# Attention outputs in five circulating PSUM banks, and the clamp of the first 24 weight tiles on GpSimd

## The chip, the cores and the metric

The kernel runs on one core of a Trainium2 chip, as one launch. The metric is the device time of that core in microseconds (us), the median of three runs.

## What is computed

The reference, cut to its core (NumPy, float32 inputs except where noted below):

```python
# attention: batch 4, heads 8, 512 local tokens, 32 global tokens, head size 64, window 32
def sm(s):
    e = np.exp(s - np.max(s, axis=-1, keepdims=True))
    return e / (np.sum(e, axis=-1, keepdims=True) + 1e-09)
s_g = scale * q_g @ concat(k_g, k_l).T            # a global token sees everything
out_g = sm(s_g) @ concat(v_g, v_l)
s_ll = where(abs(pos_q - pos_k) <= 32, scale * q_l @ k_l.T, -1e9)
s_l = concat(scale * q_l @ k_g.T, s_ll)           # a local token sees its window and the globals
out_l = sm(s_l) @ concat(v_g, v_l)
x = heads_to_columns(concat(out_g, out_l))        # 2176 tokens x 512
h = max(x @ w1, x @ w2, x @ w3)                   # 512 -> 768
x = h @ w_out                                     # 768 -> 512
g = softplus(x @ w_in2)                           # 512 -> 2048
out = g @ w_out2                                  # 2048 -> 512
```

The weights are float64 arrays. The kernel reads them as pairs of 32-bit integers, puts them together into float32 on the chip ("decoding"), and then splits each float32 number into a high part that TensorE multiplies exactly and a low remainder (high and low part of weights: the two halves of `w`; of activations: `xh` and `xl`, `hh` and `hl`). A product is three matmuls: high x high, high x low, low x high.

## The kernel before

**Attention** runs in 32 chunks k, each of two heads and 256 local tokens. A chunk goes through these steps: `s1`, the scores on TensorE into a PSUM tile of two banks (`ps`, L149) and on VectorE the masked row maximum, kept as a minimum of the negated scores (L155), which also takes the scores out of PSUM; `s1e`, the exponentials on ScalarE (L162); `s1f`, the reciprocal of the sums on VectorE (L168, L169) and two normalising multiplies on GpSimd (L171, L172); `s1g`, for every other chunk, the scores of the global tokens (L184, L190); `s2`, five transposes of the attention weights on TensorE (L218, L219); `s2e`, their copies out of PSUM (L230 on ScalarE; L232 on ScalarE or L234 on VectorE); `s3`, the attention output (L245, L249); `s3h` and `s3l`, its high and low part (L259, L270) or, from the third half-batch on, a copy that goes to memory (L262). `gsoft` is the softmax of the global tokens (L202 to L208), `g2` the transposes of their weights with the copies (L279 to L285), `g3` their output (L297).

**The first dense pair** runs in eight units u of 256 or 288 tokens. A unit has 18 **up slots**: 12 matmuls each (L504 to L506) of one weight tile with `xh` and `xl`, then a copy (L515, ScalarE) or a running maximum (L518, VectorE). After three slots `split_h` makes the parts `hh` (L533) and `hl` (L536). Two **down blocks** of 36 matmuls each follow (L550 to L552). The two products of the second pair come after all of it, from about 320 us on.

**Decoding** a tile of 128 x 512 weights (`dec_stream`) takes an absolute value on ScalarE (L448), a clamp on VectorE (L462), and three integer steps on VectorE (L465, L469, L473), the first two of which write a PSUM tile `pt` as long as the tile is "staged", which the first 24 are. Then ScalarE copies the high part (L442) and GpSimd subtracts for the low part (L443).

**PSUM.** The pool `pm` has five banks that circulate: up slots, down blocks, transposes, global scores and `pt` all take the next one. The scores have two banks, and the attention outputs `po` and `pog` share one bank of their own (tag "o", L241, L292).

**Order.** Every engine works through its instructions in program order, and the program order is what the Python code writes: `att_stream` and `dec_stream` are generators that the code at L671 to L715 advances. Each yield of attention is followed by some steps of decoding (`part`, with the debts `D0`, `D2`, `D3`) and by an up slot if its weights are decoded; after that the up slots of units 0 and 1 run with `FJ` decoding steps and `RJ` attention steps each, and from unit 2 on with `RA` attention steps a slot. For the first `KS` = 8 chunks a chunk is written as one fixed sequence (L328 to L362), for the later ones ("dense attention", among up slots) as the sequence of letters in `ORD` (L364 to L404), with a yield after nearly every step. All loads from memory are issued by SyncE in the order in which the code reaches them.

## Time and profile before

| | before |
|---|---|
| median of three runs | 813.41 us (811.31 to 814.13) |
| the profiled execution | 813.12 us, its span 811.4 us |
| TensorE matmul busy | 778.8 us, 96% of the span |
| VectorE, ScalarE, GpSimd busy | 524.2 us (65%), 423.7 us (52%), 173.6 us (21%) |
| chain of work that ended last | TensorE 86%, VectorE 6%, ScalarE 3%, memory 2% |

Busy time is counted over the whole span. The program has stages with different limits: eleven attention chunks with the first decoding (to 66.5 us), the up slots of the first two units with the rest of the 24 tiles (to 119.8 us), attention and down blocks (to 155.5 us), dense attention between up slots (to about 320 us), and the dense products. The mean granted clock of TensorE over the span is 0.994 of its full speed.

### The profile page before, as it was taken

Reading aid. Unit: us, or ns where it says so; the run is one execution under the profiler, and the core shown is the slowest. Engines: PE = TensorE matmul, PEld = TensorE weight load, DVE = VectorE, ACT = ScalarE, POOL = GpSimd, SP = SyncE. Lnnn points to the kernel's source line nnn. Section 1 sums busy time; section 2 is a strip of 40 time slices with the busy share of each in tenths; the row PEclk is TensorE's granted clock in tenths of the full one; section 3 lists DMA queues with packets and bytes.
Section 4 is the critical chain, followed back from the end, with each engine's and each line's share of the span. In section 5 each row is a group of like instructions: output and inputs, shape, how many; then the busy total and the mean of one; then the engine's idle time right before and its main releaser. Section 6 shows DMA issues by size and latency. Waiting matters only on the chain.

```text
span 811.4 us, 17312 instructions
## 1 busy us (share of the span) xinstructions
PE 778.8 (96%) x6600; PEld 730.4 (90%) x6600; DVE 524.2 (65%) x1350; ACT 423.7 (52%) x1032; POOL 173.6 (21%) x183
## 2 busy tenths in 40 slices
PE   5689988999999999999998999999999999999998
PEld 3578987988989998999998889988999999999998
DVE  5867962455454453377746455655437989999996
ACT  5744534433433441324322688888878744444443
POOL 4434533211211120022223033433312200000000
PEclk9999999999999999999999999999999999999999
DMA  9827314433433411526020445544625734444421
GB/s 339 311 87 256 148 53 123 141 123 101 147 108 112 153 48 48 205 107 214 15 65 15 165 151 170 179 158 155 210 88 179 247 95 130 130 131 130 130 80 65
DMA packets 72403, 111.89 MB, mean 138 GB/s; under 512 B 9984, under 2 KB 51840, under 8 KB 72320
## 3 DMA queue, kind: packets, MB, share of 16 engines
q1 hardware_dynamic: 72320, 110.78, 40.8%
q8 instruction: 52, 0.85, 0.4%
q14 instruction: 31, 0.25, 0.1%
HBM read 80.67 MB, written 30.08 MB: 136 GB/s over the span
## 4 chain that ended last, share of the span: by engine, by line
PE 86%; DVE 6%; ACT 3%; DMA 2%; issue 1%; POOL 0%; SPq 0%; DVEq 0%; ACTq 0%; POOLq 0%
PE pu L504 8%; PE ph L976 8%; PE ph L978 8%; PE ph L977 8%; PE pu L505 7%; PE pu L506 7%; PE mb L863 7%; PE mb L864 7%; PE mb L862 7%; PE pd L550 3%; PE pd L551 3%; PE pd L552 3%; PE ps L149 2%; ACT s L162 2%; PE po L245 2%; DMA raw<-in_w_dram 2%
## 5 line engine op out<-in xcount | busy, mean ns | idle before, releaser
L504 PE MATMUL pu<-xh,w 128*128 128x288 f32 (+1 forms) x576 | 172.3, 299 | 5.3 <-DVE tmp L473 4.8
L505 PE MATMUL pu<-xl,w 128*128 128x288 f32 (+1 forms) x576 | 167.4, 291 | 0.0
L506 PE MATMUL pu<-xh,w 128*128 128x288 f32 (+1 forms) x576 | 166.7, 289 | 0.0
L863 PE MATMUL mb<-wo,oh 128*128 128x256 f32 x480 | 135.8, 283 | 0.0
L864 PE MATMUL mb<-wo,ol 128*128 128x256 f32 x480 | 135.7, 283 | 0.0
L862 PE MATMUL mb<-wo,oh 128*128 128x256 f32 x480 | 135.2, 282 | 0.0
L504 PEld LDWEIGHTS pu<-xh,w 128*128 128x128 f32 x576 | 109.6, 190 | 11.0 <-issue 5.4
L976 PE MATMUL ph<-o,w 128*128 128x384 f32 (+1 forms) x320 | 115.2, 360 | 0.5 <-ACT o L555 0.5
L978 PE MATMUL ph<-o,w 128*128 128x384 f32 (+1 forms) x320 | 115.0, 360 | 0.0
L977 PE MATMUL ph<-o,w 128*128 128x384 f32 (+1 forms) x320 | 115.0, 359 | 0.0
L505 PEld LDWEIGHTS pu<-xl,w 128*128 128x128 f32 x576 | 109.8, 191 | 0.0
L506 PEld LDWEIGHTS pu<-xh,w 128*128 128x128 f32 x576 | 109.6, 190 | 0.0
L984 DVE SCALAR_TENSOR_TENSOR g<-ph,a 128x384 f32<-128x384 f32 (+1 forms) x80 | 48.8, 610 | 88.5 <-ACT a L983 64.0
L855 ACT ACTIVATE oh<-sm 128x640 fp32r<-128x640 f32 (+1 forms) x72 | 49.8, 692 | 89.6 <-DVE sm L850 83.8
L862 PEld LDWEIGHTS mb<-wo,oh 128*128 128x128 f32 x480 | 91.7, 191 | 0.0
L864 PEld LDWEIGHTS mb<-wo,ol 128*128 128x128 f32 x480 | 91.3, 190 | 0.0
L863 PEld LDWEIGHTS mb<-wo,oh 128*128 128x128 f32 x480 | 91.2, 190 | 0.0
L162 ACT ACTIVATE s<-s,nm 128x160 f32<-128x160 f32 x128 | 53.4, 419 | 56.4 <-DVE nm L155 56.3
L443 POOL TENSOR_TENSOR w<-tmp,w 128x512 fp32r<-128x512 f32 x40 | 53.1, 1328 | 128.9 <-ACT w L442 82.5
L518 DVE TENSOR_TENSOR m<-m,pu 128x256 f32<-128x256 f32 (+1 forms) x96 | 41.7, 434 | 56.4 <-PE pu L506 50.6
L171 POOL TENSOR_TENSOR s<-s,rs 128x512 f32<-128x512 f32 x32 | 33.4, 1044 | 165.1 <-DVE rs L169 87.8
L976 PEld LDWEIGHTS ph<-o,w 128*128 128x128 f32 x320 | 60.2, 188 | 6.5 <-ACT o L555 0.7
(125 smaller groups left out, 1584.7 us busy)
## 6 DMA issues: line engine op xcount, KB each, us to landing
gl<-gd SPq DMA_DIRECT2D x32, 512.0 KB, 5.1
kq<-in_kq_dram SPq DMA_DIRECT2D x31, 448.0 KB, 4.4
raw<-in_w_out_dram SPq DMA_DIRECT2D x22, 512.0 KB, 4.1
raw<-in_w_dram SPq DMA_DIRECT2D x18, 512.0 KB, 7.6
gd<-g SPq DMA_DIRECT2D x48, 192.0 KB, 2.5
vt<-in_vw_dram SPq DMA_DIRECT2D x16, 512.0 KB, 5.5
raw<-in_w_in_dram SPq DMA_DIRECT2D x16, 512.0 KB, 7.5
gd<-g SPq DMA_DIRECT2D x32, 256.0 KB, 3.9
```

Source lines behind the costliest of these rows:

```text
L162: nc.scalar.activation(s[:, u, :], s[:, u, :], AF.Exp, scale=-1.0, bias=g["nm"][:, u:u + 1], accum_out=g["sm"][:, u:u + 1])
L443: nc.gpsimd.tensor_tensor(w[:, 1, :], tf, w[:, 0, :].bitcast(F32), op=ALU.subtract)
L504: nc.tensor.matmul(p, lhsT=w[:, 0, k], rhs=xh[:, k, 0:n], start=(k == 0), stop=False)
L505: nc.tensor.matmul(p, lhsT=w[:, 0, k], rhs=xl[:, k, 0:n], start=False, stop=False)
L506: nc.tensor.matmul(p, lhsT=w[:, 1, k], rhs=xh[:, k, 0:n], start=False, stop=(k == 3))
L855: nc.scalar.activation(oh[:, a:b], src, AF.Copy)
L862: nc.tensor.matmul(p, lhsT=oh[:, a], rhs=w[:, 0], start=st, stop=False, skip_group_check=True)
L863: nc.tensor.matmul(p, lhsT=oh[:, a], rhs=w[:, 1], start=False, stop=False, skip_group_check=True)
L864: nc.tensor.matmul(p, lhsT=ol[:, a], rhs=w[:, 0], start=False, stop=sp, skip_group_check=True)
L976: nc.tensor.matmul(p, lhsT=w[:, 0, k], rhs=oh[:, 0:n], start=(k == 0), stop=False)
L977: nc.tensor.matmul(p, lhsT=w[:, 0, k], rhs=ol[:, 0:n], start=False, stop=False)
L978: nc.tensor.matmul(p, lhsT=w[:, 1, k], rhs=oh[:, 0:n], start=False, stop=(k == 3))
```

## The change

- `po` and `pog` take the next of the five circulating banks instead of a bank of their own; the bank that this frees becomes a pool `pt` for the decoding's PSUM tile alone.
- The clamp of the 24 staged tiles runs on GpSimd, right behind the absolute value. The other 16 tiles keep theirs on VectorE. A staged tile has three yields instead of four.
- The fixed sequence holds for eleven chunks instead of eight (`KS`), and its steps stand in another order: the reciprocals and multiplies of chunk k-1 behind the scores of chunk k, the global softmax in one piece but for its scaling, and `g2` and `g3` apart from their copies (`g2e`, `g3e`).
- Dense attention is written out instead of `ORD`: scores, output and transposes directly behind one another, then the exponentials, the multiplies, and the global tokens' steps.
- `hl` runs on GpSimd for the first three tiles of unit 0 alone; before, for all of units 0 and 1.
- The numbers that set how many steps of one stream go with one of the other are set anew (two pieces of that table are shown). `warm` is removed; it was called with 0.

```diff
-    WM = 0
     KL = 10
     KW = 9
-    KS = 8
-    ORD = 'AHaBbFDIEG'
+    KS = 11
     HHA = 2
-    HLP = 2
+    HLP = 3
...
+    pt = mo_ctx.enter_context(tc.tile_pool(name="pt", bufs=1, space=PSUM))
...
-        po = pp.tile([128, 4, 64], F32, tag="o", name="po", bufs=1)
+        po = ptile([128, 4, 64], "po")
...
-        nc.vector.tensor_copy(gt[0:96, 4, :], pb[0:96])
...
+        c["gt"], c["p"] = gt, (pa, pb)
+
+    def g2e(b, s):
+        c = gs[b, s]
+        gt, (pa, pb) = c["gt"], c["p"]
+        nc.vector.tensor_copy(gt[0:96, 4, :], pb[0:96])
         nc.scalar.activation(gt[:, 0:3, :], pa[:, 0:384].rearrange("p (c n) -> p c n", n=128), AF.Copy)
         nc.vector.tensor_copy(gt[0:64, 3, :], pa[0:64, 384:512])
-        c["gt"] = gt
...
     def g3(b, s):
-        c = gs.pop((b, s))
...
-        po = pp.tile([128, 2, 32], F32, tag="o", name="pog", bufs=1)
+        po = ptile([128, 2, 32], "pog")
...
+        c["po"] = po
+
+    def g3e(b, s):
+        po = gs.pop((b, s))["po"]
...
-            soft = iter(())
-            if 1 <= k <= n and groups[k - 1][1] == 1 and groups[k - 1][2] % 2 == 1:
-                soft = gsoft()
+            gq = None
+            if 2 <= k < n + 2 and groups[k - 2][1] == 1 and groups[k - 2][2] % 2 == 1:
+                gq = groups[k - 2][0], groups[k - 2][2] // 2
...
                 if q2 is not None:
                     s2(q2)
                     p2 += 1
+                for c in late:
+                    g3(*c)
                 s1e(k, 0)
                 s1e(k, 1)
                 if q3 is not None:
                     s3h(q3)
+                if k:
+                    s1f(k - 1)
+                next(soft, None)
+                if q2 is not None:
+                    s2e(q2)
+                if gq:
+                    g2(*gq)
+                elif gpend:
+                    soft = gsoft()
+                    next(soft)
+                    next(soft)
                 yield 2 if k > 1 else 4
-                next(soft, None)
                 if q3 is not None:
                     s3l(q3)
                     p3 += 1
-                if q2 is not None:
-                    s2e(q2)
-                s1f(k)
-                next(soft, None)
-                if late:
-                    g3(*late.pop())
-                    ng += 1
                 if k % 2 == 1:
                     s1g(k)
-                next(soft, None)
-                if k >= 2:
-                    b, hf, pr = groups[k - 2]
-                    if hf == 1 and pr % 2 == 1:
-                        g2(b, pr // 2)
-                        late.append((b, pr // 2))
-                yield 3
+                for c in late:
+                    g3e(*c)
+                    ng += 1
+                late = []
+                if gq:
+                    g2e(*gq)
+                    late.append(gq)
+                yield 3 if k else 4
...
             else:
-                for c in ORD:
-                    if c in "AaBb":
-                        if k < n:
-                            (s1 if c in "AB" else s1e)(k, "AaBb".index(c) // 2)
...
-                    elif c == "D":
-                        while p3 < p2 and p3 <= k - 2:
-                            s3(p3)
-                            s3h(p3)
-                            s3l(p3)
-                            p3 += 1
-                            yield 0
-                    elif c == "F":
...
-                    elif c == "E":
-                        while p2 <= min(k - 1, n - 1):
-                            s2(p2)
-                            s2e(p2)
-                            p2 += 1
-                            yield 0
...
+                if k == KS:
+                    s1f(k - 1)
+                if k < n:
+                    s1(k, 0)
+                    s1(k, 1)
+                while p3 < p2 and p3 <= k - 2:
+                    s3(p3)
+                    s3h(p3)
+                    s3l(p3)
+                    p3 += 1
+                while p2 <= min(k - (2 if k == KS else 1), n - 1):
+                    s2(p2)
+                    s2e(p2)
+                    p2 += 1
+                yield 0
+                for i in range(2):
+                    if k < n:
+                        s1e(k, i)
+                        yield 0
+                    next(soft, None)
+                    next(soft, None)
+                if k < n:
+                    s1f(k)
+                for c in late:
+                    g3(*c)
+                if gq:
+                    g2(*gq)
+                if k < n and k % 2 == 1:
+                    s1g(k)
...
+                if gpend:
+                    soft = gsoft()
+                yield 0
...
             t = tmps[i] = dp.tile([128, 512], I32, tag="tmp", name="tmp", bufs=3)
-            nc.scalar.activation(t.bitcast(F32), raws[i][:, :, 1].bitcast(F32), AF.Abs)
+            tf = t.bitcast(F32)
+            nc.scalar.activation(tf, raws[i][:, :, 1].bitcast(F32), AF.Abs)
+            if staged:
+                nc.gpsimd.tensor_scalar(tf, tf, F_LO, F_HI, op0=ALU.max, op1=ALU.min)
...
-            nc.vector.tensor_scalar(tf, tf, F_LO, F_HI, op0=ALU.max, op1=ALU.min)
-            yield
-            t2 = ptile([128, 512], "pt").bitcast(I32) if staged else t
+            if not staged:
+                nc.vector.tensor_scalar(tf, tf, F_LO, F_HI, op0=ALU.max, op1=ALU.min)
+                yield
+            t2 = pt.tile([128, 512], F32, tag="t", name="t2").bitcast(I32) if staged else t
...
-        (nc.gpsimd if HLP > u else nc.vector).tensor_tensor(hl[:, f, 0:n], m, hh[:, f, 0:n].bitcast(F32), op=ALU.subtract)
+        (nc.gpsimd if u == 0 and f < HLP else nc.vector).tensor_tensor(hl[:, f, 0:n], m, hh[:, f, 0:n].bitcast(F32), op=ALU.subtract)
...
-        FJ = 2.3
-        AD = 5
-        D0 = 0.5
-        D2 = 2.0
-        D3 = 1.0
+        FJ = 1.75
+        AD = 3
...
-        RD = 2.0
-        RA = 1.9
+        RD = 1.4
+        RA = 1.35
...
-            if v == 2:
+            elif v == 2:
                 flush()
-                part(D2)
-            elif v == 4:
-                continue
+                part(D2 if cnt < 8 else D2L)
             elif v == 3:
-                part(D3 if cnt > 1 else 3.0)
-                for _ in range(NS):
+                part(D3 if cnt < 8 else D3L)
+                for _ in range(NS if cnt < 8 else NSL):
                     if au[0] and ready(0):
                         slot(0)
-            else:
-                part(D0)
-                if cnt > 8 and au[0] and ready(0):
-                    flush()
-                    slot(0)
-            cnt += 1
+                cnt += 1
```

The instructions of each engine, in program order, before and after, at the places on which the steps below rest (without row numbers). From about 320 us on TensorE's order is the same in both.

VectorE, at the program's start, from the last of chunk 0's row maxima on, before (`s` and `nm` are what a row maximum writes, `rs` the reciprocals, L462 is the clamp of the first weight tile, the last row chunk 1's row maximum):

```order
L155 ISA s,nm<-ps,mask 128x160
L155 ISA nm 128x1
L168 TENSOR_SCALAR rs<-sm 128x4
L169 RECIPROCAL rs<-rs 128x4
L462 TENSOR_SCALAR tmp<-tmp 128x512
L155 ISA s,nm<-ps,mask 128x160
```
and after, from the last of chunk 2's row maxima on (L148, L161, L162 are the lines of before's L155, L168, L169; `t_254` is the decoding's PSUM tile, L475 the first shift):

```order
L148 ISA s,nm<-ps,mask 128x160
L148 ISA nm 128x1
L161 TENSOR_SCALAR rs<-sm 128x4
L162 RECIPROCAL rs<-rs 128x4
L475 TENSOR_SCALAR t_254<-tmp 128x512
L148 ISA s,nm<-ps,mask 128x160
```
The clamp is gone from VectorE, the first decoding step there is the shift, and 18 more rows (the row maxima of chunks 1 and 2, and a pair of reciprocals) stand ahead of it.

GpSimd, among the up slots of the first two units, before (L443 is the low part of a decoded tile `w`, L536 the low part `hl` of a hidden tile, L171 an attention multiply):

```order
L536 TENSOR_TENSOR hl<-m,hh 128x256
L443 TENSOR_TENSOR w<-tmp,w 128x512 x3
L536 TENSOR_TENSOR hl<-m,hh 128x256
L443 TENSOR_TENSOR w<-tmp,w 128x512 x4
L171 TENSOR_TENSOR s<-s,rs 128x4x128
```
and after (L449 is L443, L457 the clamp, L546 is L536):

```order
L449 TENSOR_TENSOR w<-tmp,w 128x512
L457 TENSOR_SCALAR tmp<-tmp 128x512
L449 TENSOR_TENSOR w<-tmp,w 128x512
L457 TENSOR_SCALAR tmp<-tmp 128x512
L546 TENSOR_TENSOR hl<-m,hh 128x256
L449 TENSOR_TENSOR w<-tmp,w 128x512
L457 TENSOR_SCALAR tmp<-tmp 128x512
```
Between two subtracts there now stands a clamp, of the tile that comes two later.

GpSimd before, around the low parts of the second unit:

```order
L171 TENSOR_TENSOR s<-s,rs 128x4x128
L172 TENSOR_TENSOR sg<-s,rs 128x128
L171 TENSOR_TENSOR s<-s,rs 128x4x128
L172 TENSOR_TENSOR sg<-s,rs 128x128
L536 TENSOR_TENSOR hl<-m,hh 128x288 x6
L171 TENSOR_TENSOR s<-s,rs 128x4x128
```
and VectorE after, where these six now stand (L227 copies transposed attention weights, L114 is the low part of a later unit's input):

```order
L148 ISA s,nm<-ps,mask 128x160
L148 ISA nm 128x1
L227 COPY pwt<-pw 128x512
L546 TENSOR_TENSOR hl<-m,hh 128x288 x6
L161 TENSOR_SCALAR rs<-sm 128x4
L162 RECIPROCAL rs<-rs 128x4
L114 TENSOR_TENSOR xl<-xr,xh 128x256 x2
```
The six low parts have moved from GpSimd, behind two chunks' multiplies, to VectorE, behind one copy.

TensorE, dense attention, before (`pw`, `pg` transposes, `ps` scores, `pu` an up slot):

```order
L218 MATMUL pw<-ident,s 128x128 x4
L219 MATMUL pg<-ident,sg 128x128
L149 MATMUL ps<-kq 64x160 x8
L504 MATMUL pu<-xh,w 128x256
L505 MATMUL pu<-xl,w 128x256
L506 MATMUL pu<-xh,w 128x256
```
and after (`po` is the output of the chunk before the one whose scores are `ps`; L142, L238, L242, L211, L212 are the lines of before's L149, L245, L249, L218, L219):

```order
L142 MATMUL ps<-kq 64x160 x8
L238 MATMUL po<-pgt,vb 64x128 x4
L242 MATMUL po<-pwt,vt 64x64 x8
L211 MATMUL pw<-ident,s 128x128 x4
L212 MATMUL pg<-ident,sg 128x128
L514 MATMUL pu<-xh,w 128x256
L515 MATMUL pu<-xl,w 128x256
```
Before, transposes and scores stood together and the output four up slots later; now scores, output and transposes stand in one row ahead of the slots.

## Rows read from the trace of the kernel before

**Rows 1.** Stretches: length, busy PE, PEld, DVE, ACT, POOL (count), clock, DMA, GB/s

```profile
0.00:66.50 66.50, 47.97 (x632) 38.12 (x633) 44.95 (x173) 40.36 (x142) 26.88 (x43) 0.97 0.64 232
66.50:119.80 53.30, 48.50 (x363) 47.49 (x361) 45.31 (x86) 24.58 (x50) 27.43 (x24) 0.97 0.44 165
119.80:155.50 35.70, 32.90 (x353) 28.91 (x352) 12.22 (x54) 16.82 (x62) 10.32 (x14) 0.95 0.36 112
155.50:320.00 164.50, 163.13 (x1890) 147.69 (x1887) 80.20 (x301) 64.43 (x231) 24.82 (x34) 1.00 0.34 108
320.00:811.40 491.40, 486.33 (x3372) 468.18 (x3370) 341.48 (x740) 277.54 (x548) 84.14 (x68) 1.00 0.41 134
68.20:69.61 1.41, 1.41 (x14) 1.41 (x13) 1.34 (x3) 1.41 (x4) 1.02 (x2) 1.00 0.77 206
155.53:157.15 1.62, 1.62 (x16) 1.48 (x13) 1.14 (x9) 1.01 (x5) 0.00 (x0) 1.00 0.47 133
280.50:282.13 1.63, 1.63 (x15) 1.49 (x14) 0.69 (x1) 0.28 (x2) 1.25 (x2) 1.00 0.75 255
```

**Rows 2.** TensorE's waits, 0 to 160 us: waiter, releaser, sum, count, longest

```profile
PE ps L149 <- DVE nm L155: 5.4, 3, 2.2
PE pu L504 <- DVE tmp L473: 4.8, 4, 2.2
...
PE pd L551 <- POOL hl L536: 2.0, 1, 2.0
```

**Rows 3.** VectorE groups by shape, 0 to 120 us: busy, mean ns, idle before

```profile
L469 DVE SCALAR_TENSOR_TENSOR pt<-raw,pt 128x512 int32<-128x512 int32 x24 | 16.6, 691 | 0.4
...
L155 DVE CUSTOM_DVE_ANT_0 s<-ps,mask 128x160 f32<-128x160 f32 x44 | 11.8, 319 | 6.9 <-PE ps L149 6.9
L462 DVE TENSOR_SCALAR tmp<-tmp 128x512 f32<-128x512 f32 x24 | 10.3, 427 | 5.1 <-ACT tmp L448 5.1
...
L518 DVE TENSOR_TENSOR m<-m,pu 128x288 f32<-128x288 f32 x10 | 4.5, 447 | 0.0
```

**Rows 4.** GpSimd groups by shape, 0 to 120 us

```profile
L443 POOL TENSOR_TENSOR w<-tmp,w 128x512 fp32r<-128x512 f32 x24 | 30.9, 1289 | 35.3 <-ACT w L442 30.7 <-issue 4.6
...
L65 POOL COPY mask<-mask 128x160 f32<-128x160 f32 x1 | 0.3, 320 | 0.0
```

**Rows 5.** GpSimd's timeline: start, length, instruction, wait before it

```profile
12.47 1.04 POOL L171 TENSOR_TENSOR s<-s,rs 128x512 f32<-128x512 f32 x1 [3.16 <-DVE rs L169]
```

**Rows 6.** Chain of waits, 0 to 20 us: start, length, instruction

```profile
9.46 0.43 DVE tmp L462
...
10.16 1.76 ACT s L162 x8
```

**Rows 7.** TensorE's timeline, score matmuls of two early chunks

```profile
10.96 1.34 PE L149 MATMUL ps<-kq 64*64 64x160 f32 x16 [2.17 <-DVE nm L155]
...
31.86 0.78 PE L149 MATMUL ps<-kq 64*64 64x160 f32 x16 [0.66 <-PE pg L219]
```

**Rows 8.** ScalarE groups by shape, 0 to 120 us

```profile
L448 ACT ACTIVATE tmp<-raw 128x512 f32<-128x512 f32 x24 | 15.9, 661 | 9.9 <-DMA raw<-in_w_dram 5.2 <-DMA raw<-in_w_out_dram 4.6
L442 ACT ACTIVATE w<-tmp 128x512 fp32r<-128x512 f32 x24 | 15.0, 625 | 10.3 <-DVE tmp L473 10.3
```

**Rows 9.** VectorE's timeline: last decoding step of two weight tiles

```profile
66.47 0.66 DVE L473 SCALAR_TENSOR_TENSOR tmp<-raw,pt 128x512 int32<-128x512 int32 x1
...
115.31 0.69 DVE L473 SCALAR_TENSOR_TENSOR tmp<-raw,pt 128x512 int32<-128x512 int32 x1
```

**Rows 10.** TensorE's timeline around the second unit's first down block

```profile
137.87 0.40 PE L550 MATMUL pd<-hh,w 128*128 128x288 f32 x1 [0.62 <-ACT hh L533]
...
147.55 0.77 PE L149 MATMUL ps<-kq 64*64 64x160 f32 x16
```

**Rows 11.** GpSimd's timeline, the second unit's low parts

```profile
139.43 4.57 POOL L536 TENSOR_TENSOR hl<-m,hh 128x288 fp32r<-128x288 f32 x6
```

**Rows 12.** VectorE groups by shape, whole run: low parts

```profile
L536 DVE TENSOR_TENSOR hl<-m,hh 128x288 fp32r<-128x288 f32 x18 | 8.4, 467 | 0.6
```

More of the change, by code (lines that the diff above doesn't have):

```diff
@@ L49, in body @@
     ones = const.tile([128, 128], F32R, name="ones")
-    def warm(n):
-        if n:
-            p = ptile([128, 128], "warm")
-            for _ in range(n):
-                nc.tensor.matmul(p, lhsT=ones, rhs=ones, start=True, stop=True)
     def setup():
@@ L283, in g2 @@
             nc.tensor.transpose(pa[0:n, 128 * i:128 * i + 128], t[:, o:o + n], ident)
+        c["gt"], c["p"] = gt, (pa, pb)
[3 more added lines that the diff above has]
+        nc.vector.tensor_copy(gt[0:96, 4, :], pb[0:96])
         nc.scalar.activation(gt[:, 0:3, :], pa[:, 0:384].rearrange("p (c n) -> p c n", n=128), AF.Copy)
         nc.vector.tensor_copy(gt[0:64, 3, :], pa[0:64, 384:512])
-        c["gt"] = gt
     def g3(b, s):
-        c = gs.pop((b, s))
+        c = gs[b, s]
         gt, v0, v1 = c["gt"], c["v0"]["v"], c["v1"]["v"]
         vs = [(v0, 0, 128), (v0, 2, 128), (v1, 0, 128), (v1, 2, 64), (v1, 3, 96)]
-        po = pp.tile([128, 2, 32], F32, tag="o", name="pog", bufs=1)
+        po = ptile([128, 2, 32], "pog")
         for e in range(2):
@@ L322, in att_stream @@
         late = []
+        soft = iter(())
         p2 = p3 = um = ng = 0
         for k in range(n + 3):
-            soft = iter(())
-            if 1 <= k <= n and groups[k - 1][1] == 1 and groups[k - 1][2] % 2 == 1:
-                soft = gsoft()
+            gq = None
+            if 2 <= k < n + 2 and groups[k - 2][1] == 1 and groups[k - 2][2] % 2 == 1:
+                gq = groups[k - 2][0], groups[k - 2][2] // 2
             if k < KS:
@@ L362, in att_stream @@
-                yield 3
-            else:
-                for c in ORD:
-                    if c in "AaBb":
-                        if k < n:
-                            (s1 if c in "AB" else s1e)(k, "AaBb".index(c) // 2)
-                            if c in "ab":
-                                yield 0
-                        if c in "AB":
-                            next(soft, None)
-                    elif c == "H":
-                        if late:
-                            g3(*late.pop())
-                            ng += 1
-                            yield 0
-                    elif c == "D":
-                        while p3 < p2 and p3 <= k - 2:
-                            s3(p3)
-                            s3h(p3)
-                            s3l(p3)
-                            p3 += 1
-                            yield 0
-                    elif c == "F":
-                        if k < n:
-                            s1f(k)
-                            yield 0
-                        next(soft, None)
-                    elif c == "G":
-                        if k < n and k % 2 == 1:
-                            s1g(k)
-                            yield 0
-                    elif c == "E":
-                        while p2 <= min(k - 1, n - 1):
-                            s2(p2)
-                            s2e(p2)
-                            p2 += 1
-                            yield 0
-                    elif c == "I" and 2 <= k < n + 2:
-                        b, hf, pr = groups[k - 2]
-                        if hf == 1 and pr % 2 == 1:
-                            g2(b, pr // 2)
-                            yield 0
-                            late.append((b, pr // 2))
@@ new lines, in att_stream @@
+                for c in late:
[6 more added lines that the diff above has]
+                yield 3 if k else 4
+            else:
+                if k == KS:
[27 more added lines that the diff above has]
+                    s1g(k)
+                for c in late:
+                    g3e(*c)
+                    ng += 1
+                late = []
+                if gq:
+                    g2e(*gq)
+                    late.append(gq)
+                if gpend:
+                    soft = gsoft()
+                yield 0
@@ L611, in body @@
         nc.vector.memset(ones.bitcast(F32), 1.0)
-        warm(WM)
         setup()
@@ L615, in body @@
         cp, NC = None, 13
-        FJ = 2.3
-        AD = 5
-        D0 = 0.5
-        D2 = 2.0
-        D3 = 1.0
+        FJ = 1.75
+        AD = 3
+        D2 = 1.5
+        D3 = 0.75
         NS = 1
+        D2L = 2.25
+        D3L = 1.5
+        NSL = 2
         MG = 1
@@ L673, in body @@
                 au[0] += 1
-                continue
-            if v == 2:
+            elif v == 2:
                 flush()
-                part(D2)
-            elif v == 4:
-                continue
+                part(D2 if cnt < 8 else D2L)
             elif v == 3:
-                part(D3 if cnt > 1 else 3.0)
-                for _ in range(NS):
+                part(D3 if cnt < 8 else D3L)
+                for _ in range(NS if cnt < 8 else NSL):
                     if au[0] and ready(0):
                         slot(0)
-            else:
-                part(D0)
-                if cnt > 8 and au[0] and ready(0):
-                    flush()
-                    slot(0)
-            cnt += 1
+                cnt += 1
         flush()
```

## The prediction

> **What bounds the kernel now.** I read the stages first: busy time of every engine in five stretches of the span [rows 1]. From 155.5 us on TensorE is the bound: 163.13 of 164.5 us in the rest of the attention, 486.33 of 491.40 us after it. From 320 us on TensorE's instructions are the same before and after, so I expect nothing there. The time lies in front: TensorE is busy 47.97 of 66.5 us, 48.50 of 53.3 us and 32.90 of 35.7 us, and even its busy time there is stretched, since the mean granted clock is 0.97, 0.97 and 0.95 of full speed [rows 1]. What TensorE waits for in the first 160 us [rows 2] is mostly VectorE (the row maximum of the scores, 5.4 us; a decoded weight tile or what is queued behind it, 4.8 us) and once GpSimd (a hidden tile's low part, 2.0 us). So whatever shortens VectorE's queue before 120 us, and the GpSimd wait behind it, moves everything that follows to the left, because what follows is a full TensorE queue. VectorE itself is busy 45.31 of 53.3 us in the stretch of the up slots [rows 1].
>
> **The change part by part.** The sum is made against the profiled execution, 813.12 us (the median of the three runs is 813.41).
>
> *Clamp price.* The change takes 24 clamps of 0.427 us (10.2 us) from VectorE [rows 3] and puts 24 on GpSimd, where the trace has none. The nearest rows are GpSimd's own: a one-input copy of 160 columns takes 0.320 us, so 512 columns take at most 1.02; work with two inputs on 512 columns takes 1.289 us for a subtract [rows 4] and 1.04 for a multiply [rows 5]. A clamp reads one input, so I take 0.8 us, as the copy with a fixed part in its time, and keep 0.5 to 1.29.
> The Trainium skill's page "GPSIMD Engine Reference", section 4.1, says to give elementwise work to VectorE: GpSimd is about half as fast with two inputs and near line rate with one. By the figure of its section 3.1 (1.03 cycles an element at 1.2 GHz) 512 columns would stream in an estimated 0.44 us, and the sum would be about a microsecond better. No run here shows that operation yet.
>
> *Stage 1, 0 to 66.5 us (eleven attention chunks and the first tiles).* Before, the first clamp (at 9.46 us) waits for a weight load and stands ahead of chunk 1's row maximum, whose exponentials start at 10.16 [rows 6]; chunk 2's score matmuls wait 2.17 us for it and start at 10.96 [rows 7]. After, decoding begins behind chunk 2, VectorE takes chunk 1's scores as soon as they stand, and chunk 2 starts about 2.0 us earlier. About 1.8 us of that go back one chunk later: the first shift of a tile now waits at the head of VectorE's queue for ScalarE's copy (0.661 us [rows 8]) and GpSimd's clamp behind a multiply, with chunk 3's scores queued behind it. Chunks 2 to 6 took (31.86 - 10.96)/5 = 4.18 us each [rows 7]. VectorE's work per chunk that is no decoding stays; decoding was 0.8 of a tile at 0.427 + 3 x 0.69 = 2.5 us [rows 3], or 2.0 us, and is 0.66 of a tile (the order's rows) at 2.07, or 1.4. Five chunks at 0.63 less give 3.2 us. Two smaller things remain. The reciprocals behind the next chunk's scores take a wait for the exponentials out of VectorE's queue, and the attention output no longer waits for its one own bank; against that the global softmax's scaling stands late in chunk 7 and holds TensorE. Together I put them at 0.9. Stage 1: 2.0 - 1.8 + 3.2 + 0.9 = **4.3 us** at equal work (bounds 2 and 7).
>
> *Stage 2, the up slots (66.5 to 119.8 us).* TensorE alone needs 30 slots of 1.41 us (256 columns [rows 1]) or 1.59 (288), 45 us of the 53.3. Tiles came every (115.31 - 66.47)/16 = 3.05 us [rows 9]. After, 32 slots and 17 tiles are left here. Per tile VectorE needs 2.07 us and its maxima and three low parts (20 x 0.447 + 3 x 0.467 us [rows 3, 12], over 17 tiles), 2.7 us; GpSimd 1.289 + 0.8 = 2.1 us. And there is a new ring over two tiles, since GpSimd clamps tile i+1 behind the subtract of tile i-1: ScalarE's copy 0.625 [rows 8], subtract 1.289, clamp 0.8, VectorE 2.07 and 0.6 of maxima, handoffs 0.2, in all 5.6 or 2.8 us a tile. TensorE's 32 slots are 48 us, 2.8 a tile too. So the 3.05 give way to a draw between three engines. The last two tiles still wait for their loads, now with GpSimd's clamp in that chain: 2.7 us, where TensorE's one long wait there was 2.2 [rows 2]. The clock's mean of 0.97 over 53.3 us is 1.6 us lost, of which I keep half. With 1.9 of friction: 45 + 2.7 + 0.8 + 1.9 = 50.4 against 53.3, **2.9 us** (bounds 0 and 7).
>
> *Stage 3, the second unit's first down block.* It waits 0.62 us, starts at 137.87 and ends at 147.55 [rows 10]: 10.3 us for 36 matmuls that take 4.8 at full clock (a twelfth of a 1.59 slot each). It is fed by six low parts on GpSimd, 4.57 us in a row [rows 11], queued behind an attention multiply. After, VectorE makes them at 0.467 us each [rows 12], right behind a copy of the attention weights, so the fifth stands some 3 us after the transposes, part of it beside other matmuls, and the block loses about 1.5 instead of 5.5. **4 us** (bounds 2.5 and 5).
> A multiply of 1.04 us may run on GpSimd then [rows 5]. The Trainium skill's page "SBUF — State Buffer", section "Who interferes with whom", says that a VectorE instruction with two SBUF inputs, as these low parts have, blocks while GpSimd reads SBUF. By that rule the gain would be a microsecond smaller; the rows shown do not settle it.
>
> *Stage 4, 120 to 320 us.* TensorE is full, so only its own cost can shrink. A slot alone behind score matmuls takes 1.62 us, within a row of slots 1.41, behind the transposes of the weights 1.63 with the last transpose's own time in it [rows 1]. The change puts output and transposes directly behind the scores: by the order, runs of slots or down blocks that start behind scores, global scores or global output go from 27 to 14. 13 x 0.2 = **2.5 us** (bounds 3.5 and -1, the loss being chunks that now come too close). The split evacuation of the global transposes, the bank for decoding alone and the extra weight copies on ScalarE lie beside a full TensorE: nothing.
>
> Sum: 4.3 + 2.9 + 4 + 2.5 = 13.7, so 813.1 - 13.7 = **799.4 us**.
>
> **The rivals.**
> *A: GpSimd sets the pace.* If a clamp costs as much as the subtract (1.289), the ring is 6.1 us for two tiles, 3.05 a tile, which is where it was: stage 2 gives nothing and stage 1 loses another 1 us. 813.1 - (3.3 + 4 + 2.5) = 803.3. For it: no row of GpSimd shows 512 columns below 1.04. Against: those have two inputs. The skill's rule on elementwise work points to this case.
> *B: the tiles come from memory, not from VectorE.* If they arrive no faster than before because their loads are issued late (the change puts loads of queries, keys and values ahead of weight loads), stages 1 and 2 give 1 us together: 813.1 - (1 + 4 + 2.5) = 805.6. Against it: 165 GB/s move in stage 2 where 232 did in stage 1 [rows 1].
> *C, slower: the dense attention starts to wait.* Between a chunk's scores and its transposes there now lie about three slots, one score group and one output on TensorE, 8 to 10 us, where there were some 14. The chain through that distance is scores 0.77 [rows 10], row maximum 4 x 0.319 overlapping to about 1.1 [rows 3], exponentials 1.76 [rows 6], then 12.47 - 11.92 = 0.55 to the multiply and 1.04 in it [rows 5, 6], an estimated 0.4 for the multiply's second part, and an estimated 2.4 for a hidden tile's copy that stands ahead of the exponentials on ScalarE and waits for a slot to end: 8.0 us. That leaves 0 to 2. From 0.8 us a chunk over 18 chunks (14 us) on the whole gain is gone; at 1.2 us a chunk the time is 821. For it: the small margin. Against: ScalarE is busy only 64.43 and VectorE 80.20 of 164.5 us there [rows 1].
>
> **How the numbers follow.** Forecast 0.60, A 0.18, B 0.12, C 0.10. A measurement of this kernel tells differences of about 0.3% (2.4 us) from none. The forecast's own bounds are the sums of the bounds above, pulled in a little since all four would have to go one way: 791 and 809; A and B lie inside, C is left out. Faster by over 0.3%: nearly all of the forecast and most of A and B, 0.84; within 0.3%: 0.07; slower: 0.09, nearly all of it C.
>
> **What would show it.** Right: chunk 2's scores start near 9 us and chunk 7's near 28; the up slots end near 112; the block at 137.87 takes about 6.3 us; clamps on GpSimd near 0.8 us; slots alone behind scores almost gone from 155 us on, and TensorE still without gaps there. Wrong: clamps of 1.2 us or more with VectorE waiting for them (A); ScalarE's copies waiting for loads all through stage 2 (B); TensorE waiting ahead of transposes of the weights after 120 us (C).

## The result and the profile after

The changed kernel is slower: 818.14 us (815.33 to 818.57, 7 runs) against 811.74 us (811.05 to 814.13, 7 runs), a ratio of 1.0068 with a 95% interval of 1.0052 to 1.0084. The forecast was 799.4 us. The profiled execution took 818.42 us, its span is 816.6 us.

Stretches of the kernel after, with the columns of [rows 1]: the attention with the first tiles, the up slots from the first long run on, and dense attention from chunk 15's scores to the first slot-free down blocks. The last line is the kernel before over that third stretch.

```profile
0.00:60.00 60.00, 42.79 (x539) 32.80 (x539) 36.24 (x153) 35.85 (x130) 35.41 (x46) 0.94 0.72 262
...
62.00:121.80 59.80, 52.74 (x392) 49.63 (x388) 39.04 (x69) 25.08 (x50) 53.33 (x36) 1.00 0.35 127
...
157.60:326.79 169.19, 165.00 (x1938) 151.04 (x1938) 77.72 (x303) 63.40 (x234) 25.02 (x36) 1.00 0.35 109
```

```profile
154.80:324.06 169.26, 167.89 (x1937) 152.23 (x1937) 82.45 (x305) 65.14 (x234) 25.28 (x35) 1.00 0.34 109
```

In the up slots GpSimd (the fifth engine column) is now busy 53.33 of 59.80 us, where it was 27.43 of 53.3; VectorE has fallen to 39.04. GpSimd's groups up to 115 us say why (to be read beside [rows 4]):

```profile
L457 POOL TENSOR_SCALAR tmp<-tmp 128x512 f32<-128x512 f32 x22 | 42.3, 1921 | 2.3 <-ACT tmp L455 2.3
L449 POOL TENSOR_TENSOR w<-tmp,w 128x512 fp32r<-128x512 f32 x20 | 25.8, 1289 | 5.4 <-ACT w L448 5.4
```

The clamp takes 1.92 us there; on VectorE it took 0.43 [rows 3]. GpSimd's timeline shows clamps and subtracts end to end, 3.2 us a tile, with no wait named before most of them; VectorE's first integer step waits for the clamps over the same 59.8 us (the second fence: waiter, releaser, sum, count, longest):

```profile
83.92 1.29 POOL L449 TENSOR_TENSOR w<-tmp,w 128x512 fp32r<-128x512 f32 x1
85.18 1.91 POOL L457 TENSOR_SCALAR tmp<-tmp 128x512 f32<-128x512 f32 x1
87.06 1.26 POOL L449 TENSOR_TENSOR w<-tmp,w 128x512 fp32r<-128x512 f32 x1
88.30 1.91 POOL L457 TENSOR_SCALAR tmp<-tmp 128x512 f32<-128x512 f32 x1
90.21 1.29 POOL L449 TENSOR_TENSOR w<-tmp,w 128x512 fp32r<-128x512 f32 x1
```

```profile
DVE t L475 <- POOL tmp L457: 16.8, 13, 4.0
```

Where the time went, stage by stage, by the start of the same TensorE work in both traces (the sum is the difference of the two profiled spans, 816.6 and 811.4 us). Equal work: the long run of slots starts at 62.02 us instead of 66.53, but with two more slots to do (1.41 + 1.59 us) and one chunk's output and transposes (1.9); chunk 11's scores start at 121.76 instead of 119.81, with the 1.9 still to do.

| stage | forecast | measured |
|---|---|---|
| 1, attention and first tiles | -4.3 | -4.5 + 4.9 = +0.4 |
| 2, up slots | -2.9 | +1.95 + 1.9 - 0.4 = +3.5 |
| 3, to chunk 15's scores (154.82, now 157.62) | -4.0 | +2.8 - 3.85 = -1.1 |
| 4, to the first slot-free down blocks (324.06, now 326.79) | -2.5 | -0.1 |
| after that | 0 | +2.5 |
| sum | -13.7 | +5.2 |

### The profile page after: what moved, and what is told of

The parts are those of the page before. It is cut to its first block, busy times and chain, and to the rows that moved or that the text cites. A ratio compares the mean times of both kernels' runs of the same rounds, so it can differ in the third digit from the quotient of the medians.

```text
span 816.6 us, 17317 instructions
## 1 busy us (share of the span) xinstructions
PE 778.2 (95%) x6600; PEld 729.0 (89%) x6600; DVE 514.0 (63%) x1333; ACT 422.7 (52%) x1034; POOL 209.0 (26%) x198
## 4 chain that ended last, share of the span: by engine, by line
PE 82%; POOL 6%; DVE 6%; ACT 2%; issue 2%; DMA 1%; SPq 0%; POOLq 0%; DVEq 0%; ACTq 0%
PE ph L979 8%; PE ph L981 8%; PE ph L980 8%; PE mb L866 7%; PE mb L867 7%; PE mb L865 7%; PE pu L514 7%; PE pu L515 6%; PE pu L516 6%; POOL tmp L457 4%; PE pd L561 3%; PE pd L560 3%; PE pd L562 3%; PE ps L142 2%; PE pw L211 2%
## 5 line engine op out<-in xcount | busy, mean ns | idle before, releaser
L516 PE MATMUL pu<-xh,w 128*128 128x256 f32 (+1 forms) x576 | 167.2, 290 | 5.7 <-POOL w L449 5.5
L514 PE MATMUL pu<-xh,w 128*128 128x256 f32 (+1 forms) x576 | 170.1, 295 | 1.4 <-ACT m L525 0.9
L515 PE MATMUL pu<-xl,w 128*128 128x256 f32 (+1 forms) x576 | 166.6, 289 | 0.0
L449 POOL TENSOR_TENSOR w<-tmp,w 128x512 fp32r<-128x512 f32 x40 | 52.3, 1307 | 102.5 <-ACT w L448 52.6
L979 PEld LDWEIGHTS ph<-o,w 128*128 128x128 f32 x320 | 60.2, 188 | 6.4 <-ACT o L565 0.7
L981 PEld LDWEIGHTS ph<-o,w 128*128 128x128 f32 x320 | 60.2, 188 | 5.7
```

Of the source, the lines that this page charges most:

```text
L449: nc.gpsimd.tensor_tensor(w[:, 1, :], tf, w[:, 0, :].bitcast(F32), op=ALU.subtract)
L514: nc.tensor.matmul(p, lhsT=w[:, 0, k], rhs=xh[:, k, 0:n], start=(k == 0), stop=False)
L515: nc.tensor.matmul(p, lhsT=w[:, 0, k], rhs=xl[:, k, 0:n], start=False, stop=False)
L516: nc.tensor.matmul(p, lhsT=w[:, 1, k], rhs=xh[:, k, 0:n], start=False, stop=(k == 3))
L979: nc.tensor.matmul(p, lhsT=w[:, 0, k], rhs=oh[:, 0:n], start=(k == 0), stop=False)
L981: nc.tensor.matmul(p, lhsT=w[:, 1, k], rhs=oh[:, 0:n], start=False, stop=(k == 3))
```

## The experiments

Two theories stood at the start. G: the clamp's price on GpSimd sets the pace. W: the loss comes from the outputs in the circulating banks and the denser order of the attention. A run's time stands against runs of the kernel before on the same chip. Line numbers shift by a few from kernel to kernel.

### The clamp back on VectorE

```diff
-            if staged:
-                nc.gpsimd.tensor_scalar(tf, tf, F_LO, F_HI, op0=ALU.max, op1=ALU.min)
...
-            if not staged:
-                nc.vector.tensor_scalar(tf, tf, F_LO, F_HI, op0=ALU.max, op1=ALU.min)
+            nc.vector.tensor_scalar(tf, tf, F_LO, F_HI, op0=ALU.max, op1=ALU.min)
+            if not staged:
                 yield
```

> The kernel after, with the clamp of the 24 tiles back on VectorE, right ahead of the first shift; everything else as in the kernel after. Theory G (the clamp takes 1.92 us on GpSimd, and clamp and subtract, 3.21 us a tile, set the pace of the up slots and stand in the chain of the first chunks): the 32 slots after chunk 10 take 53 to 54 us instead of 59.8, the first stage gains about 4, the time falls by 9 to 13 us, to 805 to 809. Theory W (the loss comes from the outputs in the circulating banks and the denser order of the attention): GpSimd has time but TensorE still waits, the time falls by 3 us at most, to 815 or more.

Measured: 805.41 us against 812.56, ratio 0.9913 (0.9896 to 0.9929). Against the kernel after's 818.14 the clamp's place alone is 12.7 us (12.6 by the two ratios). The 32 slots take 51.8 us instead of 59.8, a little less than expected and at TensorE's pace:

```profile
59.20:111.00 51.80, 49.97 (x392) 48.96 (x388) 47.08 (x91) 25.06 (x50) 24.18 (x20) 1.00 0.42 152
```

The first stage gains 2.8 us, not 4: the long run of slots starts at 59.23 instead of 62.02 us. By the stages of the table above this kernel gives -2.4, -4.6, -2.9, 0 and +1.0 us, -8.9 together. G holds, W as the whole cause falls.

### The clamp alone

```diff
-            nc.scalar.activation(t.bitcast(F32), raws[i][:, :, 1].bitcast(F32), AF.Abs)
+            tf = t.bitcast(F32)
+            nc.scalar.activation(tf, raws[i][:, :, 1].bitcast(F32), AF.Abs)
+            if staged:
+                nc.gpsimd.tensor_scalar(tf, tf, F_LO, F_HI, op0=ALU.max, op1=ALU.min)
...
-            nc.vector.tensor_scalar(tf, tf, F_LO, F_HI, op0=ALU.max, op1=ALU.min)
+            if not staged:
+                nc.vector.tensor_scalar(tf, tf, F_LO, F_HI, op0=ALU.max, op1=ALU.min)
             yield
```

> The kernel before, with only the clamp of the 24 tiles moved to GpSimd, right behind the absolute value. Theory G: a tile costs GpSimd 1.29 + 1.92 us, and it has all six low parts of the first unit as well (0.74 us each), so the tiles come every 3.4 to 3.5 us instead of 3.05 and the first stage loses 2 to 4 us: 818 to 822. Theory W: VectorE is relieved of 10 us and nothing else changes, the time is that of the kernel before or up to 5 us better: 807 to 812.

Measured: 821.61 us, ratio 1.0110 (1.0091 to 1.0128). G holds for the up slots. VectorE's first integer step now waits for the clamp (18.1 us in 16 waits from 65 to 128.5 us), and 30 slots take 63 us instead of 53:

```profile
DVE pt L469 <- POOL tmp L451: 18.1, 16, 3.0
```

The first stage does not lose 2 to 4 us: the slots start at 65.42 us, 1.1 earlier than in the kernel before.

### One operation instead of two, and every second tile

```diff
-                nc.gpsimd.tensor_scalar(tf, tf, F_LO, F_HI, op0=ALU.max, op1=ALU.min)
+                nc.gpsimd.tensor_scalar(tf, tf, F_LO, None, op0=ALU.max)
```

> The kernel after, with the upper bound of GpSimd's clamp left out (one operation, the maximum with the lower bound, instead of two). If GpSimd's time goes by the number of operations (theory G with a price per operation): about 1 us instead of 1.92, GpSimd 2.3 us a tile, the up slots at TensorE's or VectorE's pace, 50 to 53 us; the time falls by 9 to 13 us, to 805 to 809. If the price does not depend on the operations: 1.9 us and 817 to 819. Theory W: 1 us or 1.9 us, the time stays at 815 or more.

Measured: 811.07 us, ratio 0.9989 (0.9978 to 1.0000). One operation takes 1.49 us, not 1, so GpSimd needs 2.8 us a tile, about as much as TensorE's slots, and the up slots take 55.4 us. The direction is G's, the fall of the price half of what I expected, and the time lies above the expected 805 to 809: the price does not go by the number of operations alone.

```profile
L457 POOL TENSOR_SCALAR tmp<-tmp 128x512 f32<-128x512 f32 x24 | 35.7, 1488 | 5.1 <-ACT tmp L455 5.1
```

```diff
-            if staged:
+            if staged and i % 2 == 1:
                 nc.gpsimd.tensor_scalar(tf, tf, F_LO, F_HI, op0=ALU.max, op1=ALU.min)
...
+            if not staged or i % 2 == 0:
+                nc.vector.tensor_scalar(tf, tf, F_LO, F_HI, op0=ALU.max, op1=ALU.min)
             if not staged:
-                nc.vector.tensor_scalar(tf, tf, F_LO, F_HI, op0=ALU.max, op1=ALU.min)
                 yield
```

> The kernel after, with the clamp of every second tile on VectorE and of the others on GpSimd. Theory G: for two tiles GpSimd needs 2 x 1.29 + 1.92 = 4.5 us, VectorE 2 x 2.07 + 0.43 + 1.2 = 5.8 us, so 2.9 us a tile, near TensorE's 2.8; the up slots take 51 to 53 us, the first stage gains about 2: 806 to 810. Theory W: 815 or more.

Measured: 812.16 us, ratio 0.9998 (0.9988 to 1.0009), the up slots 56.9 us: a miss by 2 to 6 us. My two sums by engine left out that a GpSimd clamp also stands in one tile's chain (copy, subtract, clamp, shift): in these slots VectorE's first integer step waits 7.7 us for clamps, and GpSimd's subtract 13.8 us for ScalarE's copy. The order of the four is G's: 24 clamps on GpSimd 818, 24 at a lower price 811, 12 at the full price 812, none 805.

### The price by itself

Thirty instructions on GpSimd behind everything else, all other engines idle, on the kernel with the clamp on VectorE:

```diff
+            g.tensor_copy(gb, ga)
...
+            g.tensor_scalar(gb, ga, F_LO, None, op0=ALU.max)
...
+            g.tensor_scalar(gb, ga, F_LO, F_HI, op0=ALU.max, op1=ALU.min)
...
+            g.tensor_tensor(gb, ga, ga, op=ALU.subtract)
```

> The kernel e1_clamp_vector with thirty more instructions on GpSimd behind everything else, when all other engines are idle, on scratch data: copy, maximum (one operation), maximum and minimum (two operations) and a subtract of two inputs, 128, 256 and 512 columns. If the clamp's 1.92 us is GpSimd's own price: 1.9 for two operations and 1.5 for one at 512 columns, with little that is fixed (0.5 and 0.4 at 128), the subtract 1.29 and the copy 0.9 to 1.1. If it is the company of the other engines that makes it 1.92: 0.5 to 1.0 for both here. The time itself says nothing; it is longer by what is added, some 25 us.

The time was 832.62 us. GpSimd's groups at the end:

```profile
L1033 POOL TENSOR_SCALAR gb<-ga 128x512 f32<-128x512 f32 x3 | 5.7, 1913 | 0.2
L1030 POOL TENSOR_SCALAR gb<-ga 128x512 f32<-128x512 f32 x3 | 4.4, 1483 | 0.2
L1032 POOL TENSOR_SCALAR gb<-ga 128x256 f32<-128x256 f32 x3 | 3.2, 1060 | 0.2
L1036 POOL TENSOR_TENSOR gb<-ga 128x512 f32<-128x512 f32 x3 | 3.1, 1038 | 0.2
...
L1031 POOL TENSOR_SCALAR gb<-ga 128x128 f32<-128x128 f32 x3 | 1.9, 638 | 0.2
...
L1027 POOL COPY gb<-ga 128x512 f32<-128x512 f32 x3 | 1.8, 609 | 1.3 <-DMA out_dram<-o 1.1
L1028 POOL TENSOR_SCALAR gb<-ga 128x128 f32<-128x128 f32 x3 | 1.6, 528 | 0.3
```

The 1.92 us are GpSimd's own: 1.91 with the other engines idle. The other expected prices were misses: 0.64 and 0.53 us at 128 columns instead of 0.5 and 0.4, 1.04 for the subtract instead of 1.29, 0.61 for the copy instead of 0.9 to 1.1. From 128 to 512 columns two operations cost (1.913 - 0.638)/384 = 3.3 ns a column, one (1.483 - 0.528)/384 = 2.5 ns. Here the subtract takes one tile twice; the kernel's own, of two tiles, takes 1.29 us. Arithmetic with a constant is dearer than either (1.48 and 1.91), and a copy is far cheaper; it is no measure for the clamp.

### The banks alone

```diff
+    pt = mo_ctx.enter_context(tc.tile_pool(name="pt", bufs=1, space=PSUM))
...
-        po = pp.tile([128, 4, 64], F32, tag="o", name="po", bufs=1)
+        po = ptile([128, 4, 64], "po")
...
-        po = pp.tile([128, 2, 32], F32, tag="o", name="pog", bufs=1)
+        po = ptile([128, 2, 32], "pog")
...
-            t2 = ptile([128, 512], "pt").bitcast(I32) if staged else t
+            t2 = pt.tile([128, 512], F32, tag="t", name="t2").bitcast(I32) if staged else t
```

> The kernel before, with only the outputs po and pog in the five circulating banks and the decoding's tile in a bank of its own. If the banks bound nothing here: within 1.5 us of the kernel before, 810.5 to 813.5, since the outputs' waits for their one bank (some 3 us) lie ahead of other waits. If the five banks become short (theory W): TensorE's slots wait for a free bank and the time rises by 2 us or more, to 814 or more.

Measured: 806.06 us against 812.99, ratio 0.9897 (0.9863 to 0.9932). A miss, and the largest gain of any part. Both expectations had it wrong: the banks did bind, and the change loosened them. TensorE's waits in the 30 up slots were 4.8 us in four waits for "tmp L473" [rows 2]; now they are these:

```profile
PE pu L507 <- POOL w L444: 1.6, 3, 0.9
```

A slot that waits for its weights waits for GpSimd's subtract, which writes their last part. L473 writes no weights; it is the last reader of the decoding's PSUM tile. Those four waits were for a bank. The clearest stands at 113.31 us of the kernel before, 2.18 us long, while the tile being decoded is one of the output weights, which no up slot uses; 1.5 us later TensorE's granted clock is 0.50, the lower of its two levels, for 3.4 us. The wait before the slot, and the stretches around it:

```profile
113.31 0.40 PE L504 MATMUL pu<-xh,w 128*128 128x288 f32 x1 [2.18 <-DVE tmp L473]
```

```profile
113.00:114.80 1.80, 1.49 (x11) 1.50 (x12) 1.76 (x5) 0.92 (x3) 0.80 (x1) 1.00 0.04 9
114.80:118.20 3.40, 3.40 (x16) 3.40 (x15) 1.53 (x3) 0.93 (x2) 1.77 (x2) 0.50 0.00 0
118.20:119.80 1.60, 1.60 (x13) 1.44 (x11) 0.00 (x0) 0.00 (x0) 0.00 (x0) 0.99 0.00 0
```

With the banks changed the 30 slots take 49.4 us at a clock of 1.00. That is 3.9 us of the gain; another 1.5 lie ahead of the slots, which start at 65.02 instead of 66.53 us.

Is it the decoding's own bank that helps, or one bank more in use by all? Six banks in one ring, the decoding's tile among them:

```diff
-    pm = mo_ctx.enter_context(tc.tile_pool(name="pm", bufs=5, space=PSUM))
+    pm = mo_ctx.enter_context(tc.tile_pool(name="pm", bufs=6, space=PSUM))
...
-        po = pp.tile([128, 4, 64], F32, tag="o", name="po", bufs=1)
+        po = ptile([128, 4, 64], "po")
```

> The kernel before, with the bank of the outputs added to the circulating ones: six banks that everything takes in turn, the decoding's tile too. Theory X (the slots waited for the bank that the decoding's tile held, 4.8 us and a lower clock after it; its own bank is what helped): the slots' waits for the decoding's last step are there as before, 809 to 813. Theory Y (more banks in the ring is what helped): 804 to 807.

Measured: 805.13 us against 812.75, ratio 0.9901 (0.9873 to 0.9929). X falls, Y holds: the slots' waits for the decoding's last step shrink to 0.3 us without a bank of its own, with 1.3 us of waits for running maxima beside them. The outputs had held a whole bank for a few short uses.

### The low parts of the second unit

```diff
-        (nc.gpsimd if u == 0 and f < HLP else nc.vector).tensor_tensor(hl[:, f, 0:n], m, hh[:, f, 0:n].bitcast(F32), op=ALU.subtract)
+        (nc.gpsimd if u < 2 and (u or f < HLP) else nc.vector).tensor_tensor(hl[:, f, 0:n], m, hh[:, f, 0:n].bitcast(F32), op=ALU.subtract)
```

> The kernel e1_clamp_vector, with the six low parts of the second unit back on GpSimd, as in the kernel before. If the step on the second unit's first down block was right: the block takes 9 to 10 us again instead of 5.4 and the time rises by 3 to 4.5 us, to 808.5 to 810. If the block waits for something else just as long: 805 to 806.

Measured, on the kernel with the clamp on VectorE: 808.34 us, against 805.41 without this edit on another chip (the kernel before: 812.99 and 812.56). By the two ratios it is 2.0 us more, by the times 2.9, both less than the expected 3 to 4.5. The block takes 7.2 us (133.84 to 141.07) instead of 5.4, less than the expected 9 to 10: the low parts start with the block here (133.86 us), not 1.6 us behind its start as in the kernel before.

The opposite edit on the kernel before:

```diff
-        (nc.gpsimd if HLP > u else nc.vector).tensor_tensor(hl[:, f, 0:n], m, hh[:, f, 0:n].bitcast(F32), op=ALU.subtract)
+        (nc.gpsimd if u == 0 else nc.vector).tensor_tensor(hl[:, f, 0:n], m, hh[:, f, 0:n].bitcast(F32), op=ALU.subtract)
```

> The kernel before, with the six low parts of the second unit on VectorE and nothing else changed. If the block of down matmuls behind them gains by itself: 3 to 4.5 us, 808 to 810. If what it gains is given back later: 811 to 813.

Measured: 808.08 us against 812.75, ratio 0.9945 (0.9925 to 0.9965). As expected. Then the same edit on the kernel with the banks alone:

> The kernel e8_before_banks, with the six low parts of the second unit on VectorE. If the change's parts add up (banks -6.9, low parts -2.9): 802 to 804, and then the new order of the attention and the new rates, which e1_clamp_vector has on top, cost 1 to 3 us. If the low parts gain only beside the new order: 805 to 807.

Measured: 804.03 us against 812.75, ratio 0.9894 (0.9869 to 0.9919). That is the upper edge of the first expectation; the sum of the two as measured, -6.9 and -4.7, is not reached. The kernel has neither the new order nor the new rates, and it is no slower than the one that has them and the clamp on VectorE (805.41); their intervals overlap. So order and rates together show no gain here; neither was run by itself.

### The multiply of dense attention, earlier

```diff
                     if k < n:
                         s1e(k, i)
-                        yield 0
+                        if i == 0:
+                            yield 0
...
-        RD = 1.4
-        RA = 1.35
+        RD = 1.05
+        RA = 1.0
```

> The kernel e1_clamp_vector, with the normalising multiply of dense attention written right behind the second pair of exponentials instead of a slot later, and the rates scaled so that as many slots lie between two chunks as before. If the waits of the transposes for the multiply (4.2 us in four places from 155 us on) are a question of where it stands: they go, and the time falls by 3 to 4 us, to 801 to 803. If it is the chain from the scores that is too long for the distance: the waits stay or move to VectorE's running maxima, which now stand behind a wait for the exponentials: 804.5 to 807.

Measured: 809.54 us (805.91 to 810.78), some 3 us more than without it by the two ratios (0.9952 and 0.9913), 4 by the times. The waits stay (without the edit 4.2 us, four, the longest 1.4, over the same stretch):

```profile
PE pw L211 <- POOL s L164: 4.6, 3, 2.1
```

The first expectation falls. Why the whole grew is not settled; one trace of each shows 1.8 us of it by the first slot-free down blocks (315.93 us instead of 314.15).

## Why the prediction was wrong, point by point

**The clamp's price is the step that failed.** Of the 18.7 us between forecast and result it is worth 12.7. I bounded it by 0.5 and 1.29 us and took 0.8, "as the copy with a fixed part in its time". It is 1.92. Both neighbours were of another kind: a copy, and work on two tiles. The upper end was no bound, since nothing in the trace showed that arithmetic with constants is cheaper than with two tiles. By the prediction's own ring the true price gives 5.6 + 1.1 = 6.7 us for two tiles, 3.4 a tile; GpSimd's own work alone is 1.29 + 1.92 = 3.21. Rival A named this mechanism and stopped at 1.289, so its 803.3 was too low as well. Rival B had no part: in the up slots ScalarE waits 4.5 us for loads of the output weights, and 4.6 before. With the clamp on VectorE the traces still give 8.9 us instead of 13.7: stages 1, 3 and 4 and the rest fell short by 1.9, 1.1, 2.5 and 1.0 us, and stage 2 gave 1.7 more.
The Trainium skill's page "GPSIMD Engine Reference", section 4.1, gives elementwise work to VectorE, and this case agrees: 1.92 against 0.43 us. The estimate of 0.44 us from its section 3.1 is not borne out, 1.91 us were measured with the other engines idle; nor is "roughly line-rate" for one input.

**Stage 1** ended 0.4 us behind instead of 4.3 ahead, and the clamp is only a part of that. The chain of the first 20 us shows a clamp in it, ahead of the shift and of chunk 3's row maxima:

```profile
14.03 0.56 ACT tmp L455
...
14.67 1.93 POOL tmp L457
...
16.63 0.69 DVE t L475
17.32 0.22 DVE s L148
```

The start went the way I foresaw, but by less: chunk 2's scores stand at 9.80 instead of 10.96 us, because TensorE waits 1.04 us for the load of their queries and keys, a wait for which I had no term. The lead lasts to chunk 7 (29.62 instead of 31.86 us) and is lost behind it, where chunk 8 starts at 43.67 instead of 42.58. Between them TensorE waits for the scaling of the global softmax (L201), which I had priced inside the 0.9 us of the smaller things. The transposes of its weights before (a shorter wait, for the decoding), after, and with the clamp on VectorE:

```profile
38.55 0.66 PE L283 MATMUL pa<-ident,gsc 128*128 128x128 f32 x4 [1.80 <-DVE tmp L473]
```

```profile
34.88 0.70 DVE L475 TENSOR_SCALAR t<-tmp 128x512 int32<-128x512 int32 x1 [2.30 <-POOL tmp L457]
...
38.40 0.42 PE L272 MATMUL pb<-ident,gsc 128*96 128x128 f32 x1 [5.42 <-DVE gsc L201]
```

```profile
36.60 0.28 PE L272 MATMUL pb<-ident,gsc 128*96 128x128 f32 x1 [3.87 <-DVE gsc L201]
```

A clamp holds VectorE for 2.30 us ahead of the scaling, but without it 3.87 of the 5.42 us are still there, and the clamp alone on the kernel before did not lengthen this stage. So much of this wait goes with the new order; the order was not run by itself.

**Stage 2's sum had no term for the banks.** Only stage 4 prices them, and its "the bank for decoding alone ... nothing" was wrong by some 7 us in the kernel's favour, and the 4.8 us of [rows 2] that I put down to a decoded tile and VectorE's queue were waits for a bank. Relief of VectorE, on which stages 1 and 2 rested, is not what the kernel wanted: with the clamp left on VectorE, which is then busy 47.08 of 51.80 us in the slots, these stages give 7.0 us (chunk 11's scores at 110.95 us: -8.86 + 1.9). That is about the 7.2 that I forecast, but without the relief from which I had it.

**Stage 3** was right in its part: the block at 137.87 us takes 5.4 us (145.05 to 150.46) instead of 9.7, a gain of 4.3. But between chunk 11 and the blocks TensorE waits anew, 3.3 us in three waits, which leaves about the 1.1 measured:

```profile
PE pw L211 <- DVE m L528: 1.3, 1, 1.3
PE po L238 <- DVE m L528: 1.2, 1, 1.2
...
PE pw L211 <- POOL s L164: 0.8, 1, 0.8
```

Outputs and transposes read no running maximum; by the reading above, the first two are again waits for a bank that a slot's maximum gives back. The maxima are late because VectorE waits 4.00 us for a clamp ahead of them:

```profile
121.15 0.70 DVE L475 TENSOR_SCALAR t<-tmp 128x512 int32<-128x512 int32 x1 [4.00 <-POOL tmp L457]
```

With the clamp on VectorE the first shrinks to 0.7 us and the second is gone. So theory W had a small part: with a bank of their own the outputs could not have waited these 1.2 us for a slot.

**Stage 4** had the right mechanism on both sides. TensorE's own work fell by 167.89 - 165.00 = 2.9 us (forecast 2.5), and rival C's wait came, in four of the chunks, for 4.2 us where all waits had been 1.4: together nothing. In one of them the reciprocals stand on VectorE behind a slot's maximum and the parts of a hidden tile, the multiply behind them, the transposes behind that:

```profile
205.84 0.42 DVE L528 TENSOR_TENSOR m<-m,pu 128x256 f32<-128x256 f32 x1 [0.93 <-PE pu L516]
...
206.97 0.16 DVE L161 TENSOR_SCALAR rs<-sm 128x4 f32<-128x4 f32 x1
...
207.52 1.04 POOL L164 TENSOR_TENSOR s<-s,rs 128x512 f32<-128x512 f32 x1 [6.43 <-DVE rs L162]
...
208.61 0.66 PE L211 MATMUL pw<-ident,s 128*128 128x128 f32 x4 [1.05 <-POOL s L164]
```

**The rest was not nothing.** TensorE's order is the same, but the decoding of the second 16 tiles stands a step later on VectorE, and a hidden tile's low part there now falls beside GpSimd's subtract:

```profile
436.98 1.36 POOL L449 TENSOR_TENSOR w<-tmp,w 128x512 fp32r<-128x512 f32 x1
437.22 1.43 DVE L546 TENSOR_TENSOR hl<-m,hh 128x288 fp32r<-128x288 f32 x1
...
443.11 0.46 DVE L546 TENSOR_TENSOR hl<-m,hh 128x288 fp32r<-128x288 f32 x1
```

The same instruction takes 1.43 us there and 0.46 us alone, and in the down block behind it TensorE waits 2.3 us for the hidden tile's parts (1.9 and 0.4), where it waited 1.4. The Trainium skill's page "SBUF — State Buffer", section "Who interferes with whom", has the rule that I left open in stage 3, that VectorE blocks for its second SBUF input while GpSimd reads; these rows agree with it. Not every row does: beside a clamp of GpSimd, which reads SBUF too, three low parts in the up slots take the 0.43 us that they take alone. One of them:

```profile
91.47 1.92 POOL L457 TENSOR_SCALAR tmp<-tmp 128x512 f32<-128x512 f32 x1
```

```profile
92.70 0.43 DVE L546 TENSOR_TENSOR hl<-m,hh 128x256 fp32r<-128x256 f32 x1 [0.48 <-ACT hh L543]
```

In stage 3's block nothing ran on GpSimd beside the six low parts, and they took 2.30 us; on the kernel with the banks and the low parts alone a multiply did, and they took 3.35.

Another 1.5 us are the clock: behind the wait, 444.0 to 447.5 us run at a granted clock of 0.52, and from the end of the wait to the next product's first matmul it is 8.23 us instead of 6.72. The kernel with the clamp on VectorE has the same wait, a clock of 1.00 behind it and 6.70 us, so the lower clock does not come with this wait every time.

## What to carry to other kernels

Before moving work to another engine, find a row of the same kind of instruction on that engine, or measure one; a copy and a subtract did not bracket a clamp. When TensorE waits to write a PSUM tile, see whether the releaser writes its operands or reads a PSUM tile: the second is a wait for a bank, and a bank given back to the ring was worth 7 us here, while the new order and rates together showed no gain. And split a bundle of edits: here two parts gained 8.7 us and a third lost more than that (9 us alone, 12.7 in the bundle).

## What was not expected of the hardware

On GpSimd, 128 x 512 float32 elements took 0.61 us to copy, 1.04 to subtract from themselves, 1.48 for one operation with a constant and 1.91 for two, all with the other engines idle; beside their work the clamp took the same 1.92. A VectorE subtract of two SBUF tiles took 1.43 us (288 columns) beside a GpSimd subtract instead of 0.46, and kept its 0.43 us (256 columns) beside a GpSimd clamp.
